# Moving the last tile's score work and two output rows between VectorE and TensorE in a decode step, with the last maximum and a row sum in other places

## The chip, the cores and the metric

One core of a Trainium2 chip. The metric is the device time of one execution in microseconds (us); smaller is better. Times are medians of several executions; the profile is of one execution more. TensorE (PE in the profile, PEld for its weight loads) does matmuls and transposes, VectorE is DVE, ScalarE is ACT, GpSimd is POOL, and SyncE (SP) issues most of the transfers.

## The reference

One token of a gated mix: an attention block over a cache of 4096 keys and values, and a small dense block with a squared ReLU.

```python
g = sigmoid((x * gate_w).sum(-1, keepdims=True))        # x: 1 x 1 x 512
q = (x @ wq).reshape(1, 1, 32, 128).transpose(0, 2, 1, 3)
scores = einsum("bhqd,bhkd->bhqk", q, k_cache) * 128 ** -0.5   # 32 heads, 4096 keys, 128 wide
a = einsum("bhqk,bhkd->bhqd", softmax(scores), v_cache)
a = a.transpose(0, 2, 1, 3).reshape(1, 1, 4096) @ wo           # wo: 4096 x 512
h = relu(x @ w1 + b1) ** 2                                     # 1376 wide
b = h @ w2 + b2
out = g * a + (1 - g) * b                                      # 1 x 1 x 512
```

All inputs are bf16. Keys and values are 32 MiB each, wq and wo 4 MiB each, w1 and w2 1.4 MB each.

## The kernel before

**Tiles.** The 32 heads make NT = 8 tiles of R = 4 heads. A tile's keys lie as 128 partitions (four heads of 32 partitions) by B = 128 blocks of 128 numbers, 4 MiB; the values likewise. A tile is worked in U = 4 units, so there are NU = 32 units. Five slots of 4 MiB (`ring`) take the loads in the order k0 k1 k2 v0 k3 v1 ... k7 v5 v6 m v7, where m holds w1, w2 and, later, the last four heads of wo. SP issues a load when its slot is free: a key slot when VectorE and TensorE have read that tile's keys, a value slot when the value matmuls have. The last two tiles' values come in four parts with a semaphore each (PARTS, L59); those of the last tile hold blocks 0 to 40, 40 to 76, 76 to 108 and 108 to 128.

**Scores.** Each unit has 32 key blocks. XB = 20 of them go to VectorE: a multiply with the broadcast query and a sum along the row (`ttr`, L708, L717, two instructions for a block). YB = 12 go to TensorE in two halves of HB = 6: transposes into PSUM (`transposes`, L508), a copy to SBUF on ScalarE (`evac`, L414), and a matmul with the query column (`scores`, L523). `sc_copy` (L421) copies these scores beside VectorE's into S.

**Softmax.** `smax` (L724, VectorE) takes the maximum along each row of S, `max_rows` (L530, TensorE) transposes it, `gmax` (L731, L734, VectorE) takes the maximum per head, `max_cols` (L535, TensorE) spreads it over the partitions, and `exps` (L433, ScalarE) makes the exponentials E and the row sums RS. `den` (L563) sums RS over the partitions, `recip` (L741) inverts it. `pv(u)` (L554) multiplies a unit's values with E; `norm` (L747) scales the result by the gate and the inverse sum.

**The end.** When tiles 0 to 6 (28 heads) have their results, `turn_a` (L568) transposes them, VectorE copies that to oA (L808), `spread_a` (L575) orders it for wo's layout, and VectorE copies it twice (o2A L810, o2f L811). wo lies in W as 32 rows of 512 for each partition. TP = 20 of the rows go to TensorE (`out_a`, L584, four matmuls for a row), TV = 12 to VectorE (`rows_v`, L768 to L784), which adds row times scalar into the fp32 tile `vsum`; after TM = 6 rows it does the bias and the square of the dense block (`mlp_bias`, `mlp`, L757 to L766). `mlp_h` (L599) and `mlp_out` (L611) are the dense block's matmuls. `add_v` (L590) adds vsum, summed over the partitions, to the same accumulator `acc`, and `out_b` (L620) the last four heads with wo from m's slot. L820 adds the dense block's part, and a transpose (L675), a copy (L822) and a transfer (L342) end the kernel.

**Order.** Every engine works through its own list in the order written; between engines only semaphores order the work. On TensorE the unit loop (L630) runs transposes and scores of unit i, and `PV[i]` says which units' value matmuls come in step i. At step 32 it does units 22 to 26 and then `max_rows(7)`, at step 33 `max_cols(7)` and unit 27, the last of the seventh tile (counted from one). Then come, by L661 to L673, turn_a, spread_a, out_a, mlp_h, the last den, mlp_out, units 28 to 31 with add_v ahead of unit 30, out_b. On VectorE the list ends with the last tile's ttr, norm(2), recip(3), smax(7), gmax(7), norm(3), the copies, rows_v, recip(4), norm(4) (L788 to L822). "The last second part" of the change's words is unit 29, part 1 of the last tile's values.

Of the kernel before, what the change touches and what calls it, by code (L numbers as in the profile page):

```python
# [5 lines left out]
def bass_gated_mix__gqa_block_cached__dense_activation_squared_relu__decode_kernel(  # L6
# [30 lines left out]
    R = 4  # L37
# [3 lines left out]

    U = 4
    NU = NT * U
    XB = 20
    YB = 12
    HB = YB // 2
    XT = U * XB
    LAG = 2 * U + 3

    PV = {i: [i - LAG] for i in range(LAG, LAG + (NT - 3) * U)}  # L50
# [3 lines left out]
    for i in (28, 29, 30):  # L54
        del PV[i]
    PV[NU - 2] = [NU - 3 * U, NU - 3 * U + 1]
    PV[NU] = list(range(NU - 3 * U + 2, NU - 2 * U + 3))

    PARTS = {NT - 3: [0, 64, B], NT - 2: [0, 32, 64, 96, B], NT - 1: [0, 40, 76, 108, B]}  # L59

# [10 lines left out]
    NZ = NH - NA  # L71
    TS = [0, 3, NZ]

    TV = 12
    TP = 32 - TV
    TM = 6
    INNER, OUTER, SEAM, WRAP = range(4)
# [54 lines left out]
    with ctx:  # L132
# [37 lines left out]
        xb = early(128, 4 * 128).rearrange("p (t n) -> p t n", t=4)  # L170

        qb = sb("qb", [128, NT, 128], bf16)
        kT = sb("kT", [128, NC, HB * 128], bf16)
        xcol = sb("xcol", [128, 4], bf16)
        xcolf = sb("xcolf", [128, 4], fp32)
        b1c = sb("b1c", [128, FG + 1], fp32)
# [26 lines left out]
        b2g = sb("b2g", [128, 4], fp32)  # L203
        fin = sb("fin", [128, 4], bf16)

        KP = [pb(f"KP{i}", [128, HB * 128], bf16) for i in range(3)]
        pS = pb("pS", [128, 512], fp32)
        pM = pb("pM", [128, 512], fp32)
        pO = pb("pO", [128, 512], fp32)
        pX = pb("pX", [128, 512], fp32)  # L210
        pQ = pb("pQ", [128, 512], fp32)
        S2 = [pS[:, 0:U * YB * R], pQ[:, 0:U * YB * R]]
        O2A = pS[:, 0:32]
        MT = pM[:, 0:128]
        MB = pM[:, 128:128 + NT]
# [172 lines left out]
        @block.scalar  # L388
        def _(eng):
            eng.dma_start(xrow, A_x[0, :, :]).then_inc(s_x, 16)  # L390
            eng.dma_start(grow, gate_w.rearrange("(a n) -> a n", a=1)).then_inc(s_x, 16)
            eng.dma_start(b1r, B_b1.rearrange("(a n) -> a n", a=1)).then_inc(s_b, 16)
            eng.dma_start(b2r, B_b2.rearrange("(j p) -> j p", p=128)).then_inc(s_b, 16)
            eng.wait_ge(s_xc, 1)
            eng.activation(xcolf[:, :], XC, ACT.Copy).then_inc(s_xf, 1)
            eng.wait_ge(s_xf, 1)
            eng.activation(xcol[:, :], xcolf[:, :], ACT.Copy).then_inc(s_xf, 1)
            eng.wait_ge(s_z, 1)
            eng.activation(ez[:, :], Z, ACT.Exp, scale=-1.0).then_inc(s_ez, 1)

            def qb_copy(c):
                eng.wait_ge(s_qps, c + 1)
                for r in range(R):
                    rows = slice(P * r, P * r + P)
                    eng.activation(qb[rows, c, :], QR[c % 2][rows, r * 128:r * 128 + 128], ACT.Copy)\
                       .then_inc(s_qb, 1)

            def evac(u):
                for j in range(2):
                    n = 2 * u + j  # L410
                    if n >= NC:
                        eng.wait_ge(s_sh, n - NC + 1)
                    eng.wait_ge(s_t, n + 1)
                    eng.activation(kT[:, n % NC, :],  # L414
                                   KP[n % 3][:, :], ACT.Copy).then_inc(s_ev, 1)

            def sc_copy(j):
                eng.wait_ge(s_sh, 2 * U * (j + 1))
                for r in range(R):
                    rows = slice(P * r, P * r + P)  # L420
                    eng.activation(S[rows, j % NS, XT:B], S2[j % 2][rows, r::R], ACT.Copy).then_inc(s_cp, 1)  # L421

            def exps(j):
                eng.wait_ge(s_mb, j + 1)
                eng.activation(nM[:, j:j + 1], MB[:, j:j + 1], ACT.Copy).then_inc(s_nm, 1)  # L425
                eng.wait_ge(s_nm, j + 1)
                if j == 0:
                    eng.wait_ge(s_cst, 3)
                if j >= NE:
                    eng.wait_ge(s_pv, U * (j - NE + 1))  # L430
                for r in range(R):
                    rows = slice(P * r, P * r + P)
                    eng.activation(E[rows, j % NE, :, r], S[rows, j % NS, :], ACT.Exp,  # L433
                                   bias=nM[rows, j:j + 1], scale=SCALE,
                                   accum_out=RS[rows, R * j + r:R * j + r + 1]).then_inc(s_e, 1)

            for c in range(EARLY):
                qb_copy(c)
            for i in range(NU + 2):
                if i >= U and i % U == 0:  # L440
                    sc_copy(i // U - 1)
                if i < NU:
                    evac(i)
                if i == NU - U:
                    exps(NT - 2)
                if EARLY + i < NT:
                    qb_copy(EARLY + i)
                if i > U and i % U == 1 and i != NU - U + 1:
                    exps(i // U - 1)
# [3 lines left out]
        def _(eng):  # L453
# [42 lines left out]
            def transposes(u):  # L496
                j, w = u // U, u % U
                if w == 0:
                    landed(eng, "k", j)
                for k in range(2):  # L500
                    n = 2 * u + k
                    if n >= 3:
                        eng.wait_ge(s_ev, n - 2)
                    if n == 2:
                        eng.wait_ge(s_g, 4)
                    for y in range(HB):
                        b = XT + w * YB + k * HB + y
                        mm = eng.transpose(KP[n % 3][:, y * 128:(y + 1) * 128],  # L508
                                           held("k", j)[:, b * 128:(b + 1) * 128], ident[:, :])
                    mm.then_inc(s_t, 1)  # L510

            def scores(u):
                j, w = u // U, u % U
                if w == 0:
                    if j >= 2:
                        eng.wait_ge(s_cp, R * (j - 1))
                    eng.wait_ge(s_qc, j + 1)
                for k in range(2):
                    n = 2 * u + k
                    eng.wait_ge(s_ev, n + 1)  # L520
                    for y in range(HB):
                        c = (w * YB + k * HB + y) * R
                        mm = eng.matmul(S2[j % 2][:, c:c + R], kT[:, n % NC, y * 128:(y + 1) * 128],  # L523
                                        qcol[:, R * j:R * j + R], start=True, stop=True)
                    mm.then_inc(s_sh, 1)
# [104 lines left out]
            for i in range(NU + 2):  # L630
                if i >= U and i % U == 0 and i <= NU:
                    scores(i - 1)
                if i == NU - U:
                    max_rows(NT - 2)
                    max_cols(NT - 2)
                if i < NU:
                    transposes(i)
                if i % U and i < NU:
                    scores(i - 1)
                if EARLY + i <= NT:  # L640
                    q_cols(EARLY + i - 1)
                if EARLY + i < NT:
                    q_rows(EARLY + i)
                if i == NU:
                    for u in PV.pop(i):
                        if u == (NT - 2) * U:
                            den(NG - 2)
                        pv(u)
                if i >= U and i % U == 0 and i != NU - U and i <= NU:
                    max_rows(i // U - 1)  # L650
                if i == NU + 1:
                    max_cols(NT - 1)
                    for u in range((NT - 1) * U - 1, (NT - 1) * U):
                        pv(u)
                if i > U and i % U == 1 and i < NU - U:
                    max_cols(i // U - 1)
                for u in PV.get(i, []):
                    pv(u)
                if i >= 12 and (i - 12) % 8 == 0 and (i - 12) // 8 < NG - 2:
                    den((i - 12) // 8)  # L660
            turn_a()  # L661
            spread_a()
            out_a()
            mlp_h()
            den(NG - 1)
            mlp_out()
            for u in range((NT - 1) * U, NU):
                if u == NU - 2:
                    add_v()
                pv(u)  # L670
            eng.wait_ge(s_on, NG)
# [7 lines left out]
        def _(eng):  # L679
# [28 lines left out]
            def ttr(u):  # L708
                j, w = u // U, u % U
                if w == 0:  # L710
                    landed(eng, "k", j)
                    eng.wait_ge(s_qb, R * (j + 1))
                    if j >= NS:
                        eng.wait_ge(s_e, R * (j - NS + 1))
                for b in range(w * XB, (w + 1) * XB):
                    kb = held("k", j)[:, b * 128:(b + 1) * 128]
                    ins = eng.tensor_tensor_reduce(kb, kb, qb[:, j, :], 1.0, 0.0,  # L717
                                                   ALU.mult, ALU.add, S[:, j % NS, b:b + 1])
# [69 lines left out]
            for i in range(NU + 1):  # L788
                if i == NU:
                    norm(NG - 3)  # L790
                    recip(NG - 2)
                if i >= U and i % U == 0:
                    smax(i // U - 1)
                if i == NU - U:
                    gmax(NT - 2)
                if i < NU:
                    ttr(i)
                if i >= U and i % U == 0 and i != NU - U:
                    gmax(i // U - 1)
                if EARLY + i <= NT:  # L800
                    qcol_copy(EARLY + i - 1)
# [2 lines left out]
                if i >= LAG + 1 and (i - LAG - 1) % 8 == 7 and i < NU:  # L804
                    norm((i - LAG - 1) // 8)
            norm(NG - 2)
            eng.wait_ge(s_at, 1)
            eng.tensor_copy(oA, KP[0][0:NA, 0:128]).then_inc(s_ac, 1)  # L808
            eng.wait_ge(s_at, 2)
            eng.tensor_copy(o2A[:, :], O2A).then_inc(s_ac, 1)  # L810
            eng.tensor_copy(o2f[:, :], O2A[:, TP:32]).then_inc(s_ac, 1)  # L811
            rows_v()
            recip(NG - 1)
            eng.wait_ge(s_mo, 1)
# [39 lines left out]
```

## Time and profile before

| what | value |
|---|---|
| median of three executions | 193.84 us (193.66 to 194.28) |
| the profiled execution | 194.1 us |
| its span, first to last instruction | 192.7 us |
| VectorE busy | 157.3 us, 82% |
| TensorE matmuls busy | 111.8 us, 58% |
| ScalarE busy | 84.4 us, 44% |
| bytes moved | 78.71 MB, mean 408 GB/s |
| rows of wo on VectorE (L782) | 11 x 0.751 us |
| mean granted TensorE clock | 0.584 |

The page is of one core: busy times are sums over the span, and idle time of an engine that nobody waits for costs nothing. The DMA strip gives 40 equal slices of the span, 9 meaning 90% or more. The end of the execution, put together from the timeline of each engine (start and length in us):

| start | length | engine and line | what |
|---|---|---|---|
| 151.88 | 17.08 | DVE L717 | the last tile's 80 key blocks |
| 168.96 | 0.22 | DVE L747 | norm(2) |
| 169.10 | 0.17 | DVE L741 | recip(3) |
| 169.19 | 0.25 | DVE L724 | smax(7) |
| 170.45 | 0.49 | DVE L731, L734 | gmax(7) |
| 171.54 | 1.01 | PE L554 | unit 27 |
| 172.67 | 0.22 | DVE L747 | norm(3) |
| 173.54 | 0.28 | PE L575 | spread_a |
| 174.10 | 2.30 | PE L584 | out_a |
| 174.16 | 4.42 | DVE L778, L782 | six rows |
| 176.26 | 2.82 | PE L599 | mlp_h |
| 179.67 | 4.68 | DVE L782 | six rows |
| 179.91 | 1.31 | PE L611 | mlp_out |
| 181.67 | 1.23 | PE L554 | unit 28 |

### The profile page before, as it was taken

The numbers are of one execution on the slowest core, as the hardware profiler recorded it, in microseconds if no ns is written. First come the engines' busy times: TensorE is split into PE (matmuls) and PEld (weight loads), VectorE is DVE, ScalarE is ACT, GpSimd is POOL, SyncE is SP. The second block draws the span as 40 slices with busy tenths as digits, with TensorE's granted clock in tenths as the row PEclk, the third lists the DMA queues.
The fourth block names the chain that finished last, engine by engine and source line by source line (L and its number), as shares of the span: only waits on it lengthen the run. The fifth ranks groups of instructions, "written<-read, shape, count | busy, mean of one in ns | idle before, by whom it ended". The sixth has DMA issues, their size and how long they took to land.

```text
span 192.7 us, 6055 instructions
## 1 busy us (share of the span) xinstructions
PE 111.8 (58%) x2082; PEld 99.3 (52%) x2082; DVE 157.3 (82%) x1357; ACT 84.4 (44%) x204; POOL 22.6 (12%) x56
## 2 busy tenths in 40 slices
PE   0129665545604644396569055925886489769755
PEld 0123343435503543296559045924876378658754
DVE  0220399999999999899999998998999799938821
ACT  2004776734833753087349132933644295031000
POOL 7760001994000000000000000000000000000000
PEclk9999998555555555555555555555555555555555
DMA  6999999999999999999999999999999999999990
GB/s 218 436 435 435 435 437 425 437 468 400 429 427 415 408 451 425 432 410 432 429 424 408 425 434 422 430 434 435 432 420 408 422 410 413 429 415 377 418 367 31
DMA packets 5456, 78.71 MB, mean 408 GB/s; under 512 B 1285, under 2 KB 1895, under 8 KB 2024
## 3 DMA queue, kind: packets, MB, share of 16 engines
q1 hardware_dynamic: 4452, 75.37, 92.6%
q0 software_dynamic: 960, 2.95, 3.9%
q8 instruction: 16, 0.26, 0.6%
q14 instruction: 14, 0.11, 0.1%
q10 hardware_dynamic: 14, 0.01, 0.0%
HBM read 78.32 MB, written 0.00 MB: 406 GB/s over the span
## 4 chain that ended last, share of the span: by engine, by line
DVE 48%; DMA 42%; PE 5%; SPq 2%; issue 2%; DVEq 0%
DVE ring L717 44%; DMA ring<-in_A_k_cache_dram 26%; DMA ring<-in_A_v_cache_dram 16%; PE pO L554 2%; DVE S L717 2%; PE pQ L590 1%; SPq L330 1%; PE KP L508 1%; SPq L336 1%; DVE gm L731 1%; DVE gx L734 0%; PE pQ L620 0%; PE pM L535 0%; PE pM L563 0%; SPq L337 0%
## 5 line engine op out<-in xcount | busy, mean ns | idle before, releaser
L717 DVE CUSTOM_DVE_ANT_0 ring<-ring,qb 128x128 bf16<-128x128 bf16 x640 | 137.2, 280 | 2.6 <-DMA ring<-in_A_k_cache_dram 2.6
L414 ACT ACTIVATE kT<-KP 128x768 bf16<-128x768 bf16 x64 | 48.1, 810 | 49.2 <-PE KP L508 48.8
L508 PE MATMUL KP<-ident,ring 128*128 128x128 bf16 x384 | 45.1, 302 | 23.2 <-DMA ring<-in_A_k_cache_dram 20.5
L508 PEld LDWEIGHTS KP<-ident,ring 128*128 128x128 bf16 x384 | 37.6, 140 | 25.4 <-DMA ring<-in_A_k_cache_dram 20.9
L717 DVE DVE_READ_ACCUMULATOR2_ANT S<- 128x1 f32 x640 | 48.8, 76 | 0.1
L554 PE MATMUL pO<-E,ring 128*128 128x4 bf16 x640 | 19.7, 166 | 4.0 <-DMA ring<-in_A_v_cache_dram 3.0
L554 PEld LDWEIGHTS pO<-E,ring 128*128 128x128 bf16 x640 | 18.9, 105 | 4.5 <-DMA ring<-in_A_v_cache_dram 3.2
L433 ACT ACTIVATE E<-S,nM 32x128 bf16<-32x128 f32 x32 | 18.5, 578 | 0.9
L554 PE MATMUL pX<-E,ring 128*128 128x4 bf16 x384 | 12.0, 167 | 1.6 <-DMA ring<-in_A_v_cache_dram 1.5
L554 PEld LDWEIGHTS pX<-E,ring 128*128 128x128 bf16 x384 | 11.6, 105 | 2.0 <-DMA ring<-in_A_v_cache_dram 1.8
L530 PE MATMUL pM<-identf,mp 128*1 128x128 f32 x8 | 3.1, 384 | 12.8 <-DVE mp L724 12.8
L535 PE MATMUL pM<-onesf,gx 1*128 1x1 f32 x16 | 4.7, 358 | 9.5 <-DVE gx L734 9.5
L535 PEld LDWEIGHTS pM<-onesf,gx 1*128 1x128 f32 x16 | 4.0, 307 | 10.5 <-DVE gx L734 10.5
L523 PE MATMUL pQ<-qcol,kT 128*128 128x4 bf16 x192 | 8.3, 169 | 1.1 <-ACT kT L414 1.1
L523 PEld LDWEIGHTS pQ<-qcol,kT 128*128 128x128 bf16 x192 | 8.0, 110 | 1.4 <-ACT kT L414 1.3
L782 DVE SCALAR_TENSOR_TENSOR ring<-W,o2f,ring 128x512 f32<-128x512 bf16 x11 | 8.3, 751 | 0.4
L425 ACT ACTIVATE nM<-pM 128x1 f32<-128x1 f32 x8 | 1.4, 171 | 15.6 <-PE pM L535 15.6
L433 ACT ACTIVATION_READ_ACCUMULATOR E<-S,nM 32x1 f32 x32 | 8.1, 252 | 0.0
L377 POOL DMA_DIRECT2D W<-in_A_wo_dram x14 | 8.0, 574 | 0.0
L530 PEld LDWEIGHTS pM<-identf,mp 128*1 128x1 f32 x8 | 0.7, 92 | 13.9 <-DVE mp L724 13.9
L523 PE MATMUL pS<-qcol,kT 128*128 128x4 bf16 x192 | 7.9, 168 | 0.0
L385 POOL MEMSET tick<- 1x1 f32 x1 | 0.1, 89 | 66.6 <-DMA W<-in_A_wo_dram 66.6
(83 smaller groups left out, 97.6 us busy)
## 6 DMA issues: line engine op xcount, KB each, us to landing
ring<-in_A_k_cache_dram SPq DMA_DIRECT2D x8, 4096.0 KB, 30.5
ring<-in_A_v_cache_dram SPq DMA_DIRECT2D x5, 4096.0 KB, 29.8
ring<-in_A_v_cache_dram SPq DMA_DIRECT2D x5, 1024.0 KB, 28.5
W<-in_A_wq_dram SPq DMA_DIRECT2D x1, 4096.0 KB, 12.5
ring<-in_A_v_cache_dram SPq DMA_DIRECT2D x2, 2048.0 KB, 27.8
W<-in_A_wo_dram POOLq DMA_DIRECT2D x2, 768.0 KB, 18.1
ring<-in_B_w_dram SPq DMA_DIRECT2D x1, 1376.0 KB, 24.8
ring<-in_B_w_dram SPq DMA_DIRECT2D x1, 1280.0 KB, 27.9
```

What stands on the lines that cost most here:

```text
L330: eng.dma_start(held("v", j)[:, part], v_v[j][:, part]).then_inc(s_vl[j, w], 16)
L336: eng.dma_start(held("m")[:, W2:W3], w2_v).then_inc(s_w[1], 16)
L377: eng.dma_start(W[p:p + st * (k - 1) + 1:st, :], woa_v[q:q + k, :], max_dma_last_dim=16384).then_inc(s_wp[n], 16)
L414: eng.activation(kT[:, n % NC, :], KP[n % 3][:, :], ACT.Copy).then_inc(s_ev, 1)
L433: eng.activation(E[rows, j % NE, :, r], S[rows, j % NS, :], ACT.Exp, bias=nM[rows, j:j + 1], scale=SCALE, accum_out=RS[rows, R * j + r:R * ...
L508: mm = eng.transpose(KP[n % 3][:, y * 128:(y + 1) * 128], held("k", j)[:, b * 128:(b + 1) * 128], ident[:, :])
L523: mm = eng.matmul(S2[j % 2][:, c:c + R], kT[:, n % NC, y * 128:(y + 1) * 128], qcol[:, R * j:R * j + R], start=True, stop=True)
L530: eng.transpose(MT[0:1, :], mp[:, j:j + 1], identf[:, :]).then_inc(s_mt, 1)
L535: eng.matmul(MB[:, j:j + 1], gx[0:1, j % 2, :], onesf[0:1, 0:1], start=True, stop=True).then_inc(s_mb, 1)
L554: mm = eng.matmul(O(R * j, R * j + R), held("v", j)[:, b * 128:(b + 1) * 128], E[:, j % NE, b, :], start=(b == 0), stop=(b == B - 1), skip ...
L717: ins = eng.tensor_tensor_reduce(kb, kb, qb[:, j, :], 1.0, 0.0, ALU.mult, ALU.add, S[:, j % NS, b:b + 1])
L782: eng.scalar_tensor_tensor(out=vsum[:, :], in0=wo_sb[:, TP + t, :], scalar=o2f[:, t:t + 1], in1=vsum[:, :], op0=ALU.mult, op1=ALU.add).the ...
```

## The change

- The last tile has 24 blocks of each unit's 32 on VectorE and 8, in halves of 4, on TensorE; the other tiles stay at 20 and 12. XB, YB, HB and XT become lists by tile; the PSUM and SBUF tiles stay at the largest size.
- Ten rows of wo instead of twelve are on VectorE, 22 instead of 20 on TensorE.
- max_rows and max_cols of the last tile, and smax and gmax on VectorE, leave the unit loop. On TensorE max_rows(7) stands behind turn_a and max_cols(7) behind out_a; unit 27 follows unit 26 at once. On VectorE smax(7) stands behind norm(3), and gmax(7) behind the copies and ahead of rows_v.
- add_v stands ahead of unit 29 instead of unit 30.

```diff
-    XB = 20
-    YB = 12
-    HB = YB // 2
-    XT = U * XB
+    XB = [20] * (NT - 1) + [24]
+    YB = [B // U - x for x in XB]
+    HB = [y // 2 for y in YB]
+    XT = [U * x for x in XB]
+    HM = max(HB)
...
-    PV[NU] = list(range(NU - 3 * U + 2, NU - 2 * U + 3))
+    PV[NU] = list(range(NU - 3 * U + 2, NU - U))
...
-    TV = 12
+    TV = 10
...
-                    eng.activation(kT[:, n % NC, :],
-                                   KP[n % 3][:, :], ACT.Copy).then_inc(s_ev, 1)
+                    eng.activation(kT[:, n % NC, 0:HB[u // U] * 128],
+                                   KP[n % 3][:, 0:HB[u // U] * 128], ACT.Copy).then_inc(s_ev, 1)
...
-                    for y in range(HB):
-                        b = XT + w * YB + k * HB + y
+                    for y in range(HB[j]):
+                        b = XT[j] + w * YB[j] + k * HB[j] + y
...
-                if i >= U and i % U == 0 and i != NU - U and i <= NU:
+                if i >= U and i % U == 0 and i < NU - U:
                     max_rows(i // U - 1)
-                if i == NU + 1:
-                    max_cols(NT - 1)
-                    for u in range((NT - 1) * U - 1, (NT - 1) * U):
-                        pv(u)
...
             turn_a()
+            max_rows(NT - 1)
             spread_a()
             out_a()
+            max_cols(NT - 1)
             mlp_h()
             den(NG - 1)
             mlp_out()
             for u in range((NT - 1) * U, NU):
-                if u == NU - 2:
+                if u == NU - 3:
                     add_v()
                 pv(u)
...
-                for b in range(w * XB, (w + 1) * XB):
+                for b in range(w * XB[j], (w + 1) * XB[j]):
...
-                if i >= U and i % U == 0:
+                if i >= U and i % U == 0 and i < NU:
                     smax(i // U - 1)
...
-                if i >= U and i % U == 0 and i != NU - U:
+                if i >= U and i % U == 0 and i < NU - U:
                     gmax(i // U - 1)
...
             norm(NG - 2)
+            smax(NT - 1)
             eng.wait_ge(s_at, 1)
             eng.tensor_copy(oA, KP[0][0:NA, 0:128]).then_inc(s_ac, 1)
             eng.wait_ge(s_at, 2)
             eng.tensor_copy(o2A[:, :], O2A).then_inc(s_ac, 1)
             eng.tensor_copy(o2f[:, :], O2A[:, TP:32]).then_inc(s_ac, 1)
+            gmax(NT - 1)
             rows_v()
```

More of the change, by code (lines that the diff above doesn't have):

```diff
@@ L172, in bass_gated_mix__gqa_block_cached__dense_activation_squared_relu__decode_kernel @@
         qb = sb("qb", [128, NT, 128], bf16)
-        kT = sb("kT", [128, NC, HB * 128], bf16)
+        kT = sb("kT", [128, NC, HM * 128], bf16)
         xcol = sb("xcol", [128, 4], bf16)
@@ L204, in bass_gated_mix__gqa_block_cached__dense_activation_squared_relu__decode_kernel @@
         fin = sb("fin", [128, 4], bf16)
-        KP = [pb(f"KP{i}", [128, HB * 128], bf16) for i in range(3)]
+        KP = [pb(f"KP{i}", [128, HM * 128], bf16) for i in range(3)]
         pS = pb("pS", [128, 512], fp32)
@@ L211, in bass_gated_mix__gqa_block_cached__dense_activation_squared_relu__decode_kernel @@
         pQ = pb("pQ", [128, 512], fp32)
-        S2 = [pS[:, 0:U * YB * R], pQ[:, 0:U * YB * R]]
+        S2 = [pS, pQ]
         O2A = pS[:, 0:32]
@@ L420, in sc_copy @@
                     rows = slice(P * r, P * r + P)
-                    eng.activation(S[rows, j % NS, XT:B], S2[j % 2][rows, r::R], ACT.Copy).then_inc(s_cp, 1)
+                    eng.activation(S[rows, j % NS, XT[j]:B], S2[j % 2][rows, r:U * YB[j] * R:R], ACT.Copy).then_inc(s_cp, 1)
             def exps(j):
@@ L520, in scores @@
                     eng.wait_ge(s_ev, n + 1)
-                    for y in range(HB):
-                        c = (w * YB + k * HB + y) * R
+                    for y in range(HB[j]):
+                        c = (w * YB[j] + k * HB[j] + y) * R
                         mm = eng.matmul(S2[j % 2][:, c:c + R], kT[:, n % NC, y * 128:(y + 1) * 128],
```

## The prediction

> **What bounds the kernel now.** I read the page first: the DMA strip, the queues and the costliest groups.
>
> ```profile
> span 192.7 us, 6055 instructions
> ...
> DMA  6999999999999999999999999999999999999990
> GB/s 218 436 435 435 435 437 425 437 468 400 429 427 415 408 451 425 432 410 432 429 424 408 425 434 422 430 434 435 432 420 408 422 410 413 429 415 377 418 367 31
> ...
> q8 instruction: 16, 0.26, 0.6%
> ...
> L717 DVE CUSTOM_DVE_ANT_0 ring<-ring,qb 128x128 bf16<-128x128 bf16 x640 | 137.2, 280 | 2.6 <-DMA ring<-in_A_k_cache_dram 2.6
> ```
>
> The reader is to see that the DMA engines are full in every slice but the first and the last. 78.7 MB at some 430 GB/s is the kernel; compute matters where it delays an issue, or after the last bytes. Second, the end of the chain of waits:
>
> ```profile
> 153.59 30.89 DMA ring<-in_A_v_cache_dram
> 184.47 0.05 issue
> 184.52 0.61 PE pO L554 x17
> 185.14 0.81 issue
> 185.95 0.67 PE pO L554 x19
> 186.62 1.71 PE pQ L590 x8
> 188.32 1.40 PE pO L554 x52
> ...
> 189.82 0.23 DVE onorm L747
> 190.05 0.05 issue
> 190.09 0.60 PE pQ L620 x16
> ```
>
> Part 1 of the last values lands at 184.47; then come its 36 matmuls, torn by 0.81 us in which TensorE waits for nothing shown, the row sum (L590), the last 52 matmuls, norm, out_b. Third, the issues that land after it, from the timeline of SP's queue and the DMA view of one issue at a time:
>
> ```profile
> 160.61 1.48 SPq L330 DMA_DIRECT2D ring<-in_A_v_cache_dram  x1
> ...
> 162.14 12.63 SPq L339 DMA_DIRECT2D ring<-in_A_wo_dram  x2
> ```
>
> ```profile
> ring<-in_A_v_cache_dram SPq DMA_DIRECT2D x1, 640.0 KB, 27.9
> ring<-in_A_wo_dram SPq DMA_DIRECT2D x1, 384.0 KB, 27.3
> ...
> ring<-in_A_wo_dram SPq DMA_DIRECT2D x1, 128.0 KB, 22.7
> ```
>
> Issue plus time to landing gives 160.61 + 27.9 = 188.5 for the values' last part and 162.14 + 27.3 = 189.4 for three wo heads; the last head, issued at 167.12, lands at 189.8. Part 2 (issued at 158.47, 28.5 us) lands at 187.0. This is the floor. The last 20 value matmuls cannot start before 188.50, and end at 188.5 + 20 x 0.0285 + 0.15 = 189.25 (pitch and pipeline end from the row of 52: 1.53 us). They ended at 189.71. So the most that a better order of the tail can win is **0.46 us**, and out_b then starts at 189.63, behind its first wo landing.
>
> **Part by part, on the profiled execution.** None of it touches a DMA's issue: the slots of m and the last values are freed by tile 6's keys and tile 4's values, and SP's last loads go out by 167.12 as now; nothing is moved past SP or POOL.
>
> *Sixteen more key blocks on VectorE.* From 151.88 to 168.96 it works 80 blocks, 0.2135 us each; 16 more are 3.42 us. They end at 172.38 instead of 168.96. What hides them: between 169.19 and 172.67 VectorE now has smax (0.28), gmax (0.28 + 0.21) and idle time, 3.48 us in all, because norm(3) at 172.67 waits for the seventh tile's last values (landing 171.50, matmuls 171.54 to 172.56). smax and gmax move away, so 3.42 fits in 3.48: norm(2) at 172.38, recip at 172.52, norm(3) free at 172.61. Without that cover it would be 3.4 us on the path.
>
> *Sixteen transposes and sixteen score matmuls less; evacuations of 512 instead of 768.* An evacuation now takes 0.81 us (group L414); for 512 no row exists: between 0.54 (by size) and 0.81. I take 0.54, as the cost goes with columns; nothing hangs on it, because the copies of S end at 164.1 and smax is at 172.8.
>
> *The last maximum.* max_rows now stands behind turn_a on TensorE, and spread_a, out_a and all the rest queue behind its wait for smax; smax (0.28) runs beside turn_a (0.28), so the wait is nothing. max_rows itself, 0.37, pushes spread_a from 173.54 to about 173.70 (it overlaps the 0.21 copy of oA), out_a from 174.10 to 174.27. gmax (0.5) stands ahead of rows_v, which starts at 174.83 instead of 174.16. max_cols (0.58) waits behind out_a. out_a has 88 matmuls: 88 x 0.0288 (2.30 us for 80) = 2.53, end 176.8; max_cols to 177.4; exps to 180.1 by its present 2.6 us; mlp_h (2.82) to 180.15 instead of 179.08. Behind exps wait den and part 0 of the last values: part 0 comes only at 182.3, so 2 us cover it.
>
> *Ten rows instead of twelve.* Rows cost 0.78 (4.68 for six). Six are done at 174.83 + 0.5 + 5 x 0.78 = 179.25; mlp_bias waits for mlp_h to 180.2, its three steps take 0.6, four rows 3.12: the row sum is ready at **183.9**, before at 184.35.
>
> *The row sum ahead of part 1.* add_v now waits for it with every remaining value matmul and out_b queued behind. mlp_out 181.0 to 182.3, part 0 to 183.5, add_v (1.75) 183.95 to 185.7. Part 1 landed at 184.47 and loses 1.2 us: 36 matmuls to 186.75. Part 2 waits for 186.97 and ends at 187.9; part 3 waits for 188.50. So the tail sits on the floor with 0.6 us to spare, and the span loses 0.46 us: 194.1 becomes 193.64. The profiled execution is 0.26 us above the median of 193.84. If that excess is the 0.81 us gap, the median wins only 0.2 (193.64); if it is not, 0.46 (193.38). I take the middle, **193.5**.
>
> **The gap decides.** The trace has another one on TensorE, of 0.18 us at 164.72. Between the two lie 379 weight loads, as many matmuls and ten semaphore instructions: 768, which is three times 256. The q8 queue carried 16 packets of 16 KB, 64 bytes for each of 256 instructions, and the two gaps ended 1.35 and 1.43 us after such a packet (162.35 to 163.37, 183.46 to 184.52). So TensorE stood still for its next block of instructions, and counting in 256s gives every block's beginning. From the entry into a block to the start of the next fetch it took 2.4 to 6.1 us (14 usable cases, 12 up to 4.6, then 5.5 and 6.1; the 6.1 is the one of the large gap). The Trainium skill (Runtime: NRT & Kernel Launch, Instruction fetch mechanics) has the 256-instruction blocks, but gives TensorE room for 2048 instructions and calls the crossing mostly hidden. By that no stall is left after the change and the median comes to 193.4; the trace has one fetch for each crossing and 0.81 us of standstill, so here it does not hold.
>
> The change takes 32 pairs (weight load and matmul) out of tile 7, adds 8 in out_a and moves 8 of add_v forward. So the block that began at the 18th matmul of part 1 begins at its 34th, and its fetch is asked for when the block before is entered: in mlp_h at 177.4 now, right behind mlp_h at 180.15 afterwards. Ready, by entry + (2.4 to 6.1) + 1.05 + 1.4: 185.0 to 188.75. It does no harm up to 187.5, since 35 matmuls (1.0 us) then still meet 188.50. That is a fetch up to 4.9 us after entry, 12 of 14.
>
> **Rivals.** *The fetch is late again* (slower): for it speaks that the same fetch took 6.1 us now, and that two fetches in a row are tight (the block before is entered in out_a at 174.4, ready 179.3 to 183.0, and needed at 180.2). At 6.1 us TensorE goes on at 188.65, 55 matmuls end at 190.35, 0.64 above 189.71: 194.5. With both late up to 197. Against it: the median of the fetches, 3.1 us. It decides from 187.5; it costs more than now from 188.0.
>
> *The row sum comes late* (slower): the cover for the sixteen blocks has 0.06 us to spare, and add_v now stands ahead of 88 value matmuls. From 184.75 on (0.85 later than worked out) every tenth is a tenth on the end; 1.5 us later gives 0.65 on the floor, 194.3 at least, and more with a late block. Against it: the cover counted above, and mlp_h is what mlp_bias waits for anyway.
>
> *The landings move* (faster): the last instruction packet (187.16 to 188.28) is asked for a good 1 us later and can fall behind the last values. In the trace's landing records the last of the sixteen DMA engines is 0.6 behind the next in part 3 and in both wo loads. If that packet is what holds it, all land 0.5 earlier: 193.4 - 0.5 = 192.9. Against it: the same engine is 0.6 behind in the earlier parts too.
>
> **Numbers.** A tenth of a per cent is 0.2 us, and 0.3% (0.58 us), about what a measurement of this kernel can tell from no change, is more than the floor leaves. The tail on the floor, 193.5: 0.52 (0.38 within 0.3%, 0.14 faster, as landings scatter by some tenths). Landings earlier: 0.15, faster. Late fetch: 0.25 (0.22 slower, 0.03 within). Late row sum: 0.08, slower. Faster 0.29, same 0.41, slower 0.30. The range runs from the earlier landings, 192.9, to a late block with a little more, 194.9; the forecast's own is 193.2 to 193.8.
>
> **What would show it.** Sixteen more L717 pairs up to about 172.4 and norm(3) still at 172.7; the row sum's last row near 183.9 and L590 at 184; no idle time on TensorE in front of part 1 other than the wait for the row sum; waits for the DMA ahead of the last two parts; the gap of "issue", if there, at three matmuls before part 1's end. Wrong it would be if L590 starts after 184.8, if TensorE stands for "issue" beyond 187.5, or if the values' last part lands elsewhere than at 188.5 by more than 0.3.

## The result and the profile after

The changed kernel takes **193.44 us** (median of 20 executions, 193.16 to 193.77) where the kernel before takes 194.02 (20 executions, 193.66 to 194.57): ratio 0.997, 95% interval 0.9961 to 0.9979. That is 0.58 us less. The profiled execution took 193.49 us with a span of 192.1; its lines stand at most one number off those of before (L717 is L716, L554 is L555, L590 is L591, L620 is L621).

The page, as before the DMA strip and the key blocks:

```profile
span 192.1 us, 6035 instructions
...
DMA  6999999999999999999999999999999999999991
...
L716 DVE CUSTOM_DVE_ANT_0 ring<-ring,qb 128x128 bf16<-128x128 bf16 x656 | 140.6, 283 | 2.4 <-DMA ring<-in_A_k_cache_dram 2.4
```

The DMA engines are as full as before, and VectorE does its 16 blocks more. What moved is the end. The chain of waits (start, length, what):

```profile
160.22 28.18 DMA ring<-in_A_v_cache_dram
188.40 0.05 issue
188.45 0.71 PE pO L555 x20
...
189.25 0.23 DVE onorm L746
189.48 0.06 issue
189.54 0.58 PE pQ L621 x16
```

Before, this chain hung on the landing of part 1 at 184.47 and on everything TensorE had to do after it. Now it hangs on the landing of the last part, issued at 160.22 and landed at 188.40, with only that part's 20 matmuls behind it. The same stretch on TensorE alone (start, length, idle time before and what ended it):

```profile
183.43 1.87 PE L591 MATMUL pQ<-onesf,ring 128*128 128x1 f32 x8 [0.38 <-DVE ring L781]
185.16 1.02 PE L555 MATMUL pO<-E,ring 128*128 128x4 bf16 x33
186.66 1.25 PE L555 MATMUL pO<-E,ring 128*128 128x4 bf16 x35 [0.48 <-issue]
188.45 0.69 PE L555 MATMUL pO<-E,ring 128*128 128x4 bf16 x20 [0.54 <-DMA ring<-in_A_v_cache_dram]
```

The gap that waits for nothing shown is still there, 0.48 us, and it stands behind the 33rd matmul of part 1: the block of instructions begins at the 34th. But now there is 0.54 us of waiting for the last part behind it, so it costs nothing. On VectorE:

```profile
171.95 0.22 DVE L746 SCALAR_TENSOR_TENSOR onorm<-pO,gcol,rden 128x8 bf16<-128x8 f32 x1
172.09 0.17 DVE L740 RECIPROCAL rden<-pM 128x4 f32<-128x4 f32 x1
172.47 0.22 DVE L746 SCALAR_TENSOR_TENSOR onorm<-pX,gcol,rden 128x4 bf16<-128x4 f32 x1 [0.21 <-PE pX L555]
```

norm(2) comes 3 us later than before and norm(3) still waits, 0.21 us, for the seventh tile's values: the 16 blocks lie wholly in time that was free.

### The profile page after: what moved, and what is told of

The parts are those of the page before. It is cut to its first block, busy times and chain, and to the rows that moved or that the text cites. A ratio compares the mean times of both kernels' runs of the same rounds, so it can differ in the third digit from the quotient of the medians.

```text
span 192.1 us, 6035 instructions
## 1 busy us (share of the span) xinstructions
PE 109.9 (57%) x2056; PEld 97.1 (51%) x2058; DVE 158.8 (83%) x1387; ACT 82.7 (43%) x204; POOL 22.9 (12%) x56
## 4 chain that ended last, share of the span: by engine, by line
DVE 48%; DMA 41%; SPq 6%; PE 3%; issue 1%; DVEq 0%
DVE ring L716 45%; DMA ring<-in_A_k_cache_dram 26%; DMA ring<-in_A_v_cache_dram 15%; SPq L331 5%; DVE S L716 2%; PE pO L555 1%; PE KP L509 1%; DVE gm L730 1%; DVE gx L733 0%; PE pQ L621 0%; PE pM L564 0%; PE pM L536 0%; SPq L337 0%; SPq L338 0%; SPq L294 0%
## 5 line engine op out<-in xcount | busy, mean ns | idle before, releaser
L716 DVE CUSTOM_DVE_ANT_0 ring<-ring,qb 128x128 bf16<-128x128 bf16 x656 | 140.6, 283 | 2.4 <-DMA ring<-in_A_k_cache_dram 2.4
L415 ACT ACTIVATE kT<-KP 128x768 bf16<-128x768 bf16 (+1 forms) x64 | 46.4, 783 | 48.7 <-PE KP L509 48.4
L509 PE MATMUL KP<-ident,ring 128*128 128x128 bf16 x368 | 43.0, 300 | 21.8 <-DMA ring<-in_A_k_cache_dram 18.6
L716 DVE DVE_READ_ACCUMULATOR2_ANT S<- 128x1 f32 x656 | 51.8, 79 | 0.1
L509 PEld LDWEIGHTS KP<-ident,ring 128*128 128x128 bf16 x368 | 35.6, 139 | 23.9 <-DMA ring<-in_A_k_cache_dram 19.0
L555 PE MATMUL pO<-E,ring 128*128 128x4 bf16 x640 | 19.8, 166 | 2.8 <-DMA ring<-in_A_v_cache_dram 2.2
L555 PEld LDWEIGHTS pO<-E,ring 128*128 128x128 bf16 x640 | 18.9, 105 | 3.4 <-DMA ring<-in_A_v_cache_dram 2.4
L555 PE MATMUL pX<-E,ring 128*128 128x4 bf16 x384 | 11.9, 166 | 4.7 <-DMA ring<-in_A_v_cache_dram 4.7
L555 PEld LDWEIGHTS pX<-E,ring 128*128 128x128 bf16 x384 | 11.3, 103 | 5.2 <-DMA ring<-in_A_v_cache_dram 5.1
L524 PE MATMUL pQ<-qcol,kT 128*128 128x4 bf16 x176 | 7.8, 170 | 1.0 <-ACT kT L415 0.9
L363 POOL TENSOR_SCALAR_AFFINE_SELECT selA<-selA 28x36 bf16<-28x36 bf16 (+6 forms) x22 | 7.4, 335 | 3.2 <-POOL selA L358 0.2
```

The lines of the kernel that those rows point to most:

```text
L363: eng.affine_select(out=part, in_=part, compare_op=ALU.not_equal, fill=1.0, base=-st * q, pattern=[[st, 4], [-1, st * (k - 1) + 1]], chann ...
L415: eng.activation(kT[:, n % NC, 0:HB[u // U] * 128], KP[n % 3][:, 0:HB[u // U] * 128], ACT.Copy).then_inc(s_ev, 1)
L509: mm = eng.transpose(KP[n % 3][:, y * 128:(y + 1) * 128], held("k", j)[:, b * 128:(b + 1) * 128], ident[:, :])
L555: mm = eng.matmul(O(R * j, R * j + R), held("v", j)[:, b * 128:(b + 1) * 128], E[:, j % NE, b, :], start=(b == 0), stop=(b == B - 1), skip ...
```

## The experiments

Two questions were open: whether the gap is the wait for a block of instructions and what it costs, and which part of the change wins the 0.58 us. Three theories: *block* (the excess over the landings is the wait for an instruction block, and the change wins by where it puts it), *order* (the row sum stood on the path), *share* (work taken from TensorE and ScalarE).

### The block's place, nothing else

```diff
             eng.matmul(Z, onesf[0:1, :], zp[:, :], start=True, stop=True).then_inc(s_z, 1)
+            for n in range(24):
+                eng.matmul(pS[:, 400:401], ident[:, :], ident[:, 0:1], start=True, stop=True)
```

in the kernel before, and the same with 128 and with 104. The results are not used.

> The kernel before, with 24 pairs of weight load and matmul (results unused) put at TensorE's start, where it stands idle from 9.7 to 13.2 us; nothing else. Every instruction block on TensorE then begins 24 pairs earlier in the program: the last one inside unit 28 instead of at the 18th matmul of part 1. Theory 'block' (the tail's excess over the landings is the wait for an instruction block): the wait falls into the 1.6 us in which TensorE waits for part 1 anyway, part 1 runs without a gap, the last matmuls start at the last landing; 0.4 to 0.5 us less, 193.5 to 193.6 beside 194.0, with an unchanged order. Theory 'order' (the row sum stood on the path) and theory 'share' (the work taken from TensorE and ScalarE): no change, 194.0, L591's counterpart still between parts 1 and 2 and the end at 0.5 above the floor.

> Control to the 24 pairs: the kernel before with 128 such pairs at the start, 256 instructions, one whole block. Theory 'block': the last block begins at the same matmul as before, the gap is back at the 18th matmul of part 1, and the time is that of before, 194.0 (within 0.15). If the dummy matmuls themselves did something (warm or throttle the clock, move the first issues), this kernel would show it, and more than the one with 24.

> The kernel before with 104 pairs at TensorE's start: 24 fewer than the control of 128, so the last block begins 24 pairs later than before, at the 6th of the row sum's 8 pairs, and the one ahead of it between mlp_h and mlp_out, as in the changed kernel with the row sum put back. Order and shares are those of before. Theory 'block': part 1 runs without a gap from 184.4 to 185.5, the block is there at 186.4 to 186.7 inside the row sum, part 3 starts at its landing: 193.4 to 193.6. Theory 'order' or 'share': 194.0 to 194.1, as the control.

Measured: 24 pairs 193.65 us (six executions, 193.44 to 194.26; ratio 0.9989, 0.997 to 1.0007), 128 pairs 194.08 (ratio 1.0011, 0.999 to 1.0033), 104 pairs 193.61 (twelve, 193.32 to 194.78; ratio 0.9984, 0.9968 to 0.9999). The kernel before had 194.08 and 194.12 beside them. The ratios take in the long executions, which the medians hardly feel: by them the 24 pairs are not told from no change, and the 104 only just. The chain of the control with 128:

```profile
184.17 0.61 PE pO L556 x17
184.78 1.39 issue
186.17 0.67 PE pO L556 x19
186.84 1.71 PE pQ L592 x8
```

256 instructions more and the gap is at the very same matmul, behind the 17th of part 1. Ahead of it another gap stands behind the 20th of mlp_h's 44 matmuls:

```profile
175.90 1.31 PE L601 MATMUL pX<-xcol,ring 128*128 128x1 bf16 x20
177.71 1.60 PE L601 MATMUL pX<-xcol,ring 128*128 128x1 bf16 x24 [0.50 <-issue]
```

With 24 pairs fewer than that, TensorE's timeline is:

```profile
175.93 2.79 PE L601 MATMUL pX<-xcol,ring 128*128 128x1 bf16 x44
179.82 0.59 PE L565 MATMUL pM<-RS,onesf 128*128 128x4 f32 x2 [1.09 <-issue]
...
184.26 1.12 PE L556 MATMUL pO<-E,ring 128*128 128x4 bf16 x36 [1.60 <-DMA ring<-in_A_v_cache_dram]
185.24 1.84 PE L592 MATMUL pQ<-onesf,ring 128*128 128x1 f32 x8
186.95 0.99 PE L556 MATMUL pO<-E,ring 128*128 128x4 bf16 x32
188.28 0.69 PE L556 MATMUL pO<-E,ring 128*128 128x4 bf16 x20 [0.34 <-DMA ring<-in_A_v_cache_dram]
```

Part 1 runs through, part 3 waits for its landing, and this execution took 193.42 us, as the changed kernel, in the old order and with the old shares. The gap of mlp_h has moved behind the 44th matmul, 24 pairs later; it is 1.09 us long, and the wait for part 1 covers it. So the gap follows the count of instructions: in all eleven profiled executions that have such a gap between matmuls after 175 us, of this and the other experiments, it stands ahead of the 4034th instruction recorded on TensorE or a multiple of 256 away from it (a weight load and its matmul are two). Where it sits was worth 0.47 us between the medians of 128 and of 104 pairs. But only seven of the twelve executions with 104 pairs came to 193.3 to 193.7, and the others reach 194.8; those of the changed kernel do not: a place alone is not a safe one. No long execution with 104 pairs has a profile. The profiled one with 24 pairs (194.26, the longest of its six) shows what can make one long. From its chain of waits:

```profile
169.00 0.77 PE pX L556 x23
169.77 1.06 issue
...
175.16 2.19 PE pQ L586 x76
177.34 1.10 issue
...
186.66 1.87 PE pQ L592 x8
```

And on TensorE alone, in unit 28 and up to the end of part 1:

```profile
183.34 1.02 PE L556 MATMUL pO<-E,ring 128*128 128x4 bf16 x33
184.89 1.31 PE L556 MATMUL pO<-E,ring 128*128 128x4 bf16 x43 [0.54 <-issue]
```

The last block was out of part 1, as expected: it begins behind unit 28's 33rd matmul, 24 pairs ahead of part 1's 17th. But two earlier ones now began in unit 26 and in out_a and were late by 1.06 and 1.10 us. mlp_h, the bias and VectorE's last rows came later by that, and the row sum's matmuls started at 186.66. The expectation had looked at the last block alone.

### The row sum's place

```diff
             for u in range((NT - 1) * U, NU):
-                if u == NU - 2:
+                if u == NU - 3:
                     add_v()
```

in the kernel before (first), and the reverse in the changed kernel (second).

> The kernel before with the row sum (add_v) ahead of unit 29 instead of unit 30, nothing else. Theory 'block' and theory 'order' both: the row sum runs at 184.4 to 186.1, the block that now begins at the 10th matmul of part 1 is there by then, parts 1 and 2 end at about 188.2, part 3 starts at its landing; 193.5, the whole gain of the change from this part alone. Theory 'share': no change, 194.0, since the key blocks and the wo rows stay.

> The changed kernel with the row sum back ahead of unit 30. Theory 'block': part 1 runs from its landing (184.4) without a gap, the last block begins inside the row sum and is ready at about 186.7, the row sum ends at 187.3, part 2 at 188.3, part 3 starts at its landing; as the changed kernel, 193.45 (within 0.15). Theory 'order': back to before, 193.9 to 194.0. Theory 'share': 193.45.

Measured: the row sum's move alone 193.39 us (ratio 0.9973, 0.9956 to 0.999), the changed kernel with the move undone 193.46 (0.9971, 0.9954 to 0.9988). The first, on TensorE:

```profile
184.57 1.86 PE L590 MATMUL pQ<-onesf,ring 128*128 128x1 f32 x8 [1.74 <-DVE ring L782]
186.30 1.95 PE L554 MATMUL pO<-E,ring 128*128 128x4 bf16 x68
188.46 0.69 PE L554 MATMUL pO<-E,ring 128*128 128x4 bf16 x20 [0.20 <-DMA ring<-in_A_v_cache_dram]
```

TensorE waits 1.74 us for the row sum, up to 184.57. The packet with the block's instructions ended at 184.79 in the trace's records, while the row sum's matmuls ran, and the block begins at the 10th matmul of part 1, at 186.5: with part 1 pushed back behind the row sum, the block is there in time. The second:

```profile
184.01 1.12 PE L555 MATMUL pO<-E,ring 128*128 128x4 bf16 x36 [1.41 <-DMA ring<-in_A_v_cache_dram]
184.99 1.21 PE L591 MATMUL pQ<-onesf,ring 128*128 128x1 f32 x5
186.36 0.80 PE L591 MATMUL pQ<-onesf,ring 128*128 128x1 f32 x3 [0.17 <-issue]
```

The block begins inside the row sum, as expected, at the sixth of its eight pairs, and the gap is 0.17 us. So this one move is enough for the whole gain, and with the other parts in place it isn't needed: theory order falls in its plain form, and block holds.

### The other parts

> The changed kernel with the last tile's key blocks back at 20 on VectorE and 12 on TensorE; ten rows, the last maximum and the row sum stay as changed. Theory 'block': VectorE ends its key blocks 3.4 us earlier and then waits for unit 27 as long; the last block begins at the 2nd matmul of part 1, is there at about 186, and parts 1 and 2 end at 188.0: as the changed kernel, 193.45 (within 0.15). Theory 'share' (the gain is work taken from TensorE and ScalarE): some or all of it gone, 193.7 to 194.0.

`XB = [20] * NT` in the changed kernel: 193.44 us (ratio 0.997, 0.9959 to 0.9981). As the changed kernel: beside the other parts the 16 blocks win nothing and cost nothing.

> The changed kernel with twelve wo rows on VectorE. The row sum comes 1.56 us later, 184.8, so the row sum's matmuls run 184.9 to 186.6, parts 1 and 2 end at about 188.5, just at the last landing: 193.45 to 193.6. This is the point from which a late row sum decides by the prediction (184.75). Rival 'the row sum sets the end': the whole delay comes through, 1.0 us or more, 194.4.

`TV = 12` in the changed kernel: 193.43 us (0.997, 0.9959 to 0.9982). The row sum's matmuls start 1.2 us later than in the changed kernel and nothing comes through:

```profile
184.63 1.87 PE L591 MATMUL pQ<-onesf,ring 128*128 128x1 f32 x8 [1.94 <-DVE ring L781]
186.36 2.63 PE L555 MATMUL pO<-E,ring 128*128 128x4 bf16 x88
```

All 88 matmuls run without a break, the last 20 after the landing at 188.25. Theory share falls: either share can be undone at no cost, and the row sum's move alone, with both shares as before, had the whole gain.

```diff
-    XB = [20] * (NT - 1) + [24]
+    XB = [20] * NT
...
-    TV = 10
+    TV = 12
...
-                if u == NU - 3:
+                if u == NU - 2:
                     add_v()
```

in the changed kernel leaves the last maximum's move alone; it was run twice.

> Of the change only the last maximum's new place; 20 key blocks, twelve rows and the row sum ahead of unit 30 as before. Theory 'block': the moved instructions all stand ahead of mlp_h in both kernels but for max_cols, so the last block again begins near the 18th matmul of part 1 and the gap is back, 194.0. (The row sum ready at about 185.0 instead of 184.35 adds nothing, since it is used from 186.5.) If the maximum's place gave part of the gain, 193.5 to 193.8.

> The kernel with only the last maximum moved, once more, for another profiled execution: its twelve times fell in two groups (nine at 193.2 to 193.7, three at 194.5 to 195.4), and the profiled one was of the slow group, with a gap of 1.41 us at the 18th matmul of part 1. Theory 'block': the groups differ in how soon the block's fetch starts (7.1 us after TensorE's queue reached the block ahead in the slow one); an execution at 193.2 to 193.7 has its packet ended before about 183.3, a gap of at most 0.3 us, and the last 20 matmuls at the last landing. If an execution that fast shows the same gap of 0.8 us or more in part 1, the gap isn't what separates the groups and the theory falls.

Measured: 193.53 us (twelve executions, 193.21 to 195.43; ratio 0.9985, 0.9964 to 1.0006) and 194.05 (twelve, 193.32 to 195.86; 1.0008, 0.998 to 1.0036). Both profiled executions (194.5 and 194.06) have the gap behind the 17th matmul of part 1, 1.41 and 1.17 us; the first one's chain:

```profile
184.37 0.62 PE pO L555 x17
184.98 1.41 issue
186.39 0.67 PE pO L555 x19
```

So this move leaves the gap where it was, and no steady gain was measured. Of the 24 executions 14 took 193.2 to 193.7 all the same. An execution of that length was not caught with a profile, so it isn't shown that the block was early in those.

### The floor, and the block in a worse place

> The changed kernel without the load of the last tile's blocks 108 to 128 (640 KB; unit 31 multiplies what the slot held before, and does not wait). Theory 'floor' (the tail hangs on the last landings): the wo heads land 1.5 us earlier, unit 31 follows unit 30 at once, the last 55 matmuls run from the block's arrival at 186.7 to 188.4; out_b at 188.8 instead of 189.5; 0.7 less, 192.7. Rival (TensorE's or VectorE's own work ends the kernel and the landing only coincides): at most 0.2 less, 193.25 to 193.45.

```diff
                         part = slice(PARTS[j][w] * 128, PARTS[j][w + 1] * 128)
+                        if (j, w) == (NT - 1, 3):
+                            continue
...
-                    if lo in PARTS[j]:
+                    if lo in PARTS[j] and (j, lo) != (NT - 1, 108):
```

Measured: 192.77 us (192.65 to 192.88; ratio 0.9938, 0.9925 to 0.9951), 0.67 below the changed kernel. With 640 KB less to land, the chain goes back to TensorE and to the block:

```profile
183.56 1.87 PE pQ L593 x8
185.43 0.88 PE pO L557 x33
186.31 0.46 issue
186.76 1.78 PE pO L557 x55
```

So the last landings held the end of the changed kernel (without this load the wo heads, too, land 1.5 us earlier); without them 0.46 us of gap is again on the path.

> The changed kernel with the last part of the last values cut from 20 blocks to 12 (8 more in the part ahead of it): a try at a faster kernel. Theory 'floor': the last part lands at the same 188.4, the 8 matmuls less behind it save 0.23 us up to out_b, but out_b then waits for its own landings (189.41 and 189.73 in the changed kernel): 0.05 to 0.1 less, 193.35. Rival (only the values' landing counts): 0.23 less, 193.2.

`NT - 1: [0, 40, 76, 116, B]` in PARTS of the changed kernel: 193.34 us (0.9962, 0.9952 to 0.9972). Its interval overlaps that of the changed kernel, so a gain over it isn't shown. The chain of the profiled execution (193.81, the longest of its twelve) ends as the floor theory has it, at the first wo landing instead of the values':

```profile
162.33 27.31 DMA ring<-in_A_wo_dram
189.64 0.14 issue
189.78 0.58 PE pQ L621 x16
```

> The changed kernel with 80 pairs of weight load and matmul (results unused) at TensorE's start; 128 of them cost nothing there. Theory 'block': the last two block beginnings move from behind mlp_h to the start of unit 28, and from the 34th matmul of part 1 to about the 14th of the last part. The first of them is late by up to 2 us, which pushes the row sum's stretch, and the second is asked for too late to be there by 188.8: the gap stands where nothing covers it. 0.5 to 2 us slower than the changed kernel, 194.0 to 195.5, with a gap of 'issue' inside the last 20 matmuls. Theory 'order' (the row sum's place alone makes the gain): as the changed kernel, 193.45.

80 pairs in the changed kernel: 193.59 us (twelve executions, 193.16 to 195.14; ratio 0.9984, 0.9962 to 1.0007). The expectation failed: 0.15 more than the changed kernel by the medians, not 0.5 to 2, and the interval of the ratio includes that of the changed kernel. In the profiled execution (193.76) both fetches started 3.3 us after the block ahead was entered, and no gap is left in the tail. Two of the twelve are 194.26 and 195.14, which fits late fetches, but that was not seen in a profile.

## Why the prediction was right

- **The floor.** Predicted: no order of the tail can end the last value matmuls before 189.25, 0.46 below before. Measured: they end at 189.15, with the last part landing at 188.40 instead of 188.50. Taking its 640 KB of load away made the kernel 0.67 us faster, so the last landings hold the end. By the chain of waits it is this one, and the first wo landing stands close behind it (189.41, with out_b at 189.54).
- **The sixteen blocks.** Predicted to lie in 3.48 us of cover with 0.06 to spare; norm(3) waited 0.21 us. The 96 blocks took the 20.5 us worked out; the wider margin is that tile's keys, from which VectorE started at 151.47 instead of 151.88, while the values that norm(3) waits for came only 0.2 us earlier. Undoing the sixteen changed nothing.
- **The row sum.** Predicted ready at 183.9; its matmuls started at 183.43. Of the 0.5 us some 0.2 are earlier landings (norm(3) at 172.47 instead of 172.67), 0.16 is max_rows, which delayed spread_a by less than worked out (0.87 us behind norm(3), as before, instead of 1.03), and 0.1 lies between out_a and mlp_h (2.96 us from start to start instead of 3.06). The path runs through mlp_h, as predicted: the bias waited 0.97 us for it. Twelve rows put it at 184.63, inside the 184.75 that the prediction gave as harmless, and were harmless.
- **The gap.** Predicted behind the 33rd matmul of part 1, ready 185.0 to 188.75; measured behind the 33rd, 186.66. The fetch for it started 4.1 us after the entry (180.22 to 184.30), inside the 4.9 that the prediction counted as harmless.
- **The size.** 193.5 for 193.44, but the fall is 0.58 us, not 0.34. The term that was mis-sized is the last one: the prediction took half of the 0.26 us by which the profiled execution stood above the median of three runs as the gap's. Over 20 executions the median of before is 194.02, so the profiled 194.1 was nearly a typical one, and the whole 0.46 us counted. Taken so, 194.02 - 0.46 is 193.56. The 0.46 lies within the interval of the gain, 0.41 to 0.76 us; that the landing was 0.1 earlier in the profiled execution fits the rest, but isn't shown for the others. The time itself came out so near by luck: the start was 0.18 too low and the gain 0.24 too small. And 0.41, the largest chance, went to no change within 0.3%; 0.58 us is just that, and twenty executions tell it from none.
- **What it left unsaid.** It put the gain down to the tail's order as a whole. The runs showed that the row sum's move alone gives all of it, and that the other three parts together, without that move, give all of it too: either way the last block's beginning leaves the 18th matmul of part 1. The last maximum alone gave nothing steady; the blocks and the rows were each only undone, not tried alone.
- **The rivals.** A late row sum didn't come. The fetch wasn't late by the prediction's measure (ready 186.66, harmless to 187.5), and its gap was covered. The landings moved by 0.1 us, not 0.5, and the last instruction packet isn't what holds the last of the DMA engines: by the landing records that engine was 0.61 us behind the next in part 3 before and 0.25 after, and in part 0, some 7 us earlier, 0.60 and 0.26.

## What to carry to other kernels

Take an idle stretch that waits for nothing the profile shows, and comes back after a multiple of the same count of instructions, for a wait for instructions, as it was here; count back from it to find where each block begins, and shift that place by a few instructions to see what it costs. Order moved the gap here more often than it removed it, but it can be laid into a wait that exists anyway. The arrangement with the two waits on top of each other was also the steadier one: the changed kernel's 20 executions lie within 0.61 us, the twelve with 104 pairs within 1.46, the 24 with the maximum's move within 2.65. Before sizing a gain in the tail of a kernel whose DMA is full, take the last landings as its floor, and the size from more than three runs.

## What the runs showed of the hardware

A block holds 256 instructions: 128 pairs brought the gap back to the same matmul, 24 fewer moved it by 24 pairs. The Trainium skill (Runtime: NRT & Kernel Launch, Instruction fetch mechanics) has that size, and the runs agree; it calls the crossing mostly hidden, and gaps of up to 1.41 us in the tails above disagree where the DMA is full. TensorE went on 1.3 to 1.6 us after a late block's packet had ended.

The start of a fetch was not expected to come in two kinds. With the block ahead entered at 177.5 to 177.9, it took 5.9 to 6.1 us in five profiled executions (before, 128 pairs, the row sum's move alone, the maximum's move twice), and in the one with 20 blocks, entered at 177.3, it took 3.2. Nor does the entry, from which the prediction counted, say much: in eleven of the fourteen profiled executions the packet for the tail's last block started between 183.46 and 184.55, the five above and six with the block ahead entered at 179.6 to 180.5, 2.5 us later on average, whose packets started 0.4 us later. What sets this is open; all traces have the DMA engines full at that time.

The lag of the last DMA engine behind the next was nearly the same (within 0.11 us) in all transfers of one execution from the last tile's part 0 on, and differed between executions, from 0.03 us (row sum moved back, last part landed at 188.03) to 0.79 (smaller last part, 188.66). So part of what the landings scatter by is this lag; its cause is open.
